# Key blocks of 128 within one batch, one PSUM bank per batch for the value products, maxima taken off by small products

## The chip, the cores and the metric

The kernel runs on one core of one Trainium2 chip. The time is the device time of one execution of the whole program, in microseconds; a kernel is given as the median of several runs. The engines are PE (TensorE, matrix products into PSUM), DVE (VectorE), ACT (ScalarE), POOL (GpSimd) and SP, which here only issues DMAs. PSUM is the accumulator memory in front of PE: eight banks, each of 512 fp32 values per partition, 128 partitions.

## The reference

q, k and v are float32 arrays of 8 batches x 12 heads x 448 rows x 64. The result of the attention is the input of a soft mixture of experts.

```python
scores = scale * np.matmul(q, k.transpose(0, 1, 3, 2))
m = np.max(scores, axis=-1, keepdims=True)
e = np.exp(scores - m)
attn = e / (np.sum(e, axis=-1, keepdims=True) + np.exp(-m) + 1e-09)
x = np.matmul(attn, v)          # then heads side by side: 3584 rows of 768
logits = x @ phi                # 32 slots, 4 for each of 8 experts
d = exp(logits - logits.max(0)); d /= d.sum(0) + 1e-09
slot_input = d.T @ x            # each expert: relu(slot_input @ w1) @ w2
c = exp(logits - logits.max(1)); c /= c.sum(1) + 1e-09
out = c @ slot_out
```

## The kernel before

The attention is cut into 24 units of two batches and two heads (the heads lie on the two partition halves of the transposed q and k). A row of 448 is seven blocks of 64 (TB = 7), or three of 128 and one of 64 (C3 = 3). One loop runs over steps; seven steps belong to a unit, and several units are in flight. Each step issues one score tile for the maxima of unit u (`stage_S`, L208) and, LAG = 11 steps later, one tile of transposed scores of the same unit (`stage_ST`, L242). Everything else hangs in a plan: `at(n, place, f)` puts a stage at a step, and within a step the order is "small", S, "mid", "value", ST, "end", "load" (L571 to 580). Every engine and each DMA queue works off its instructions in that written order.

The stages of a unit, with n its first step:

- `load_qk`, `load_v` (L114, L120): q and k come through POOL's queue, cast to bf16; v comes as float32 through SP's queue, two DMAs. `load_w` brings a piece of the expert weights through POOL's queue.
- `stage_T` (L194): 28 transposes of q and k of the next unit into a PSUM tile of two banks; DVE copies q (L204), then ACT copies k (L205).
- `stage_S`: four products of 64 stationary columns (two heads x two halves of 64 rows) over 448 keys; DVE reduces the two banks to row maxima (L219), which go to a tile M.
- `stage_MT` (L221, step n + 7): M is transposed by PE, copied by ACT (`mt`), exponentiated for the denominator (`em`), and POOL multiplies `mt` with a mask to `md` (L231, L237): for each batch and head a matrix of 64 x 448 whose column sum is minus the maximum of each row.
- `stage_ST`: for 64 keys of both batches, four products of a column of ones with `md` (L247) and four products of k and q (L252) add up to scores minus maxima; ACT takes the exponential (L256) into one of four buffers `et`.
- `stage_V` (L259, step n + 10): POOL casts v to bf16 beside a column of ones.
- `stage_AV` (L266): `et` times v, 64 keys of each batch at a time: 16 products of 65 columns per t, batch 0 on the upper and batch 1 on the lower row half, summed over t in a PSUM tile of two banks. AV0 gives the step of each t after n.
- `stage_AVout`, `stage_shift`, `stage_N` (L289 to L322): ACT copies the sums to the single buffer `xu` (L293, L296), POOL moves the half blocks (L304) and adds up the denominator, DVE takes reciprocals, POOL multiplies (L319).
- `stage_X` (L327, step n + 27): seven transposes, copied by DVE (L332), for the mixture's logits.

After each six units `mixture` works on the 768 features of a batch pair, in steps of its own, from 28 steps after the last of these units began. PSUM is given out by `slot` (L94): four slots of two banks, r0 to r3, each request taking the slot that is due first; the value products hold theirs from the first t to the copy. After the loop come the experts and the output (from L583).

## Time and profile before

| | |
|---|---|
| median of 3 runs | 354.83 us (351.5, 354.83, 356.85) |
| span of the profiled execution | 351.5 us |
| time of the profiled execution | equal to the lowest run, 351.5 us |
| busy: PE, DVE, POOL, ACT | 279.6, 245.8, 230.8, 223.1 us |
| one undisturbed unit (from 147.51 us on) | 9.86 us |
| main loop, last score tile | 268.75 us |
| mixture's last logits | 290.46 us |
| first output rows | 321 us |

Busy time is the union of an engine's instructions. PE's matrix products are pipelined: one row shows a product from its start to the modelled end, so the lengths of neighbours overlap, and what a group costs PE is the distance to the next start. A releaser in brackets is what ended the idle time before an instruction.

### The profile page before, as it was taken

How to read it: one execution, taken by the hardware profiler on the slowest of the kernel's cores; microseconds unless marked ns; L12 is line 12 of the kernel's file. 1: busy time of each engine (PE TensorE's matmuls, PEld its weight loads, DVE VectorE, ACT ScalarE, POOL GpSimd, SP SyncE). 2: the span in 40 equal slices, each digit the busy share in tenths (PEclk: the TensorE clock that was granted, in tenths of full speed). 3: DMA queues.
4: the chain of work that ended last, by engine and by line, in shares of the span. 5: the costliest groups of instructions: out<-in, count | busy, mean ns of one | idle time of the engine just before them, and what ended most of it. 6: DMA issues, size and time to landing. Idle time of an engine off the chain costs nothing.

```text
span 351.5 us, 14003 instructions
## 1 busy us (share of the span) xinstructions
PE 279.6 (80%) x6152; PEld 159.8 (45%) x6152; DVE 245.8 (70%) x321; ACT 223.1 (63%) x353; POOL 230.8 (66%) x413
## 2 busy tenths in 40 slices
PE   2679898998989789999968987899689745877760
PEld 1334554564555455556545544555455423342110
DVE  1886887988787978889888876878987015207440
ACT  1236887787778488888777776877588832015340
POOL 8335688899886878999876878698757573210000
PEclk9999999999999999999999999999999975596555
DMA  7455379789988898899997799869956599963997
GB/s 92 80 96 100 54 146 202 115 162 185 186 168 167 139 209 158 140 170 174 169 178 146 109 222 205 163 96 183 176 121 113 125 168 205 216 133 149 395 399 313
DMA packets 30061, 59.14 MB, mean 168 GB/s; under 512 B 4049, under 2 KB 22225, under 8 KB 30001
## 3 DMA queue, kind: packets, MB, share of 16 engines
q0 software_dynamic: 19344, 36.69, 61.7%
q1 hardware_dynamic: 10656, 21.57, 18.7%
q8 instruction: 48, 0.79, 0.9%
q14 instruction: 13, 0.10, 0.1%
HBM read 83.46 MB, written 11.01 MB: 269 GB/s over the span
## 4 chain that ended last, share of the span: by engine, by line
PE 31%; ACT 13%; DMA 12%; DVE 12%; issue 8%; POOL 6%; SPq 3%; ACTq 0%; POOLq 0%; DVEq 0%
PE ps L282 12%; ACT block L256 9%; PE ps L216 7%; DVE m L219 6%; PE ps L247 6%; DMA block<-in_moe_w_dram 5%; PE ps L252 4%; SPq L635 3%; DMA block<-in_v_dram 3%; DMA block<-in_k_dram 2%; DVE block L204 2%; DMA out_dram<-wres 2%; DVE sm L431 2%; ACT block L205 1%; POOL block L319 1%
## 5 line engine op out<-in xcount | busy, mean ns | idle before, releaser
L219 DVE TENSOR_REDUCE m<-ps 128x2 bf16<-128x896 f32 x168 | 179.5, 1090 | 41.4 <-PE ps L216 33.5
L256 ACT ACTIVATE block<-ps 128x896 bf16<-128x896 f32 x168 | 154.3, 922 | 49.9 <-PE ps L252 47.2
L216 PE MATMUL ps<-block 64*64 64x448 bf16 x672 | 66.6, 382 | 21.5 <-ACT block L205 12.0
L282 PE MATMUL ps<-block 64*128 64x65 bf16 (+1 forms) x2688 | 73.1, 196 | 4.2 <-issue 2.0
L282 PEld LDWEIGHTS <-block 64*128 64x128 bf16 (+1 forms) x2688 | 53.0, 97 | 42.6 <-issue 29.5
L247 PE MATMUL ps<-block,ones 64*64 64x448 bf16 x672 | 64.5, 364 | 5.4 <-ACT cT L445 2.4
L252 PE MATMUL ps<-block 64*64 64x448 bf16 x672 | 63.4, 356 | 0.0
L216 PEld LDWEIGHTS <-block 64*64 64x64 bf16 x672 | 32.3, 108 | 53.5 <-issue 37.4
L319 POOL TENSOR_TENSOR block<-block,rec 128x896 bf16<-128x896 f32 (+1 forms) x24 | 40.1, 1672 | 4.5 <-DVE rec L313 4.5
L304 POOL COPY block<-block 64x65 f32<-64x65 f32 x96 | 22.6, 236 | 26.5 <-ACT block L296 23.5
L231 POOL TENSOR_TENSOR block<-mt,nmask 128x768 bf16<-128x768 bf16 x24 | 36.0, 1502 | 3.9 <-ACT mt L225 2.7
L110 POOL DMA_DIRECT2D block<-in_q_dram x46 | 29.4, 640 | 14.0 <-PE ps L203 10.5
L205 ACT COPY block<-ps 128x896 bf16<-128x896 bf16 x24 | 21.8, 907 | 23.8 <-DVE block L204 23.8
L110 POOL DMA_DIRECT2D block<-in_k_dram x46 | 27.8, 618 | 2.0 <-issue 2.0
L247 PEld LDWEIGHTS <-ones 64*64 64x64 bf16 x672 | 23.5, 107 | 12.1 <-issue 7.4
L261 POOL CAST block<-block 128x896 bf16<-128x896 f32 x24 | 22.6, 941 | 5.8 <-DMA block<-in_v_dram 5.8
L203 PE MATMUL ps<-ident,block 128*64 128x128 bf16 x644 | 24.1, 228 | 2.0 <-DMA block<-in_q_dram 1.0
L203 PEld LDWEIGHTS <-block 128*64 128x64 bf16 x644 | 20.8, 115 | 8.2 <-issue 6.0
L252 PEld LDWEIGHTS <-block 64*64 64x64 bf16 x672 | 21.3, 109 | 0.9
L332 DVE COPY block<-ps 128x896 bf16<-128x896 bf16 x24 | 14.8, 616 | 9.7 <-PE ps L330 9.7
L293 ACT COPY block<-ps 128x780 f32<-128x780 f32 x24 | 19.5, 813 | 3.1 <-PE ps L282 2.0
L630 PE MATMUL ps<-wres,cT 32*128 32x384 bf16 x56 | 17.6, 493 | 4.5 <-DVE wres L633 2.5
(105 smaller groups left out, 254.4 us busy)
## 6 DMA issues: line engine op xcount, KB each, us to landing
wres<-in_moe_w_dram POOLq DMA_DIRECT2D x23, 768.0 KB, 7.7
out_dram<-wres SPq DMA_DIRECT2D x28, 384.0 KB, 4.2
block<-in_v_dram SPq DMA_DIRECT2D x46, 224.0 KB, 7.2
block<-in_moe_w_dram POOLq DMA_DIRECT2D x9, 768.0 KB, 12.8
block<-in_q_dram POOLq DMA_DIRECT2D x46, 112.0 KB, 4.8
block<-in_k_dram POOLq DMA_DIRECT2D x46, 112.0 KB, 4.5
block<-in_v_dram POOLq DMA_DIRECT2D x2, 224.0 KB, 4.2
wres<-in_q_dram POOLq DMA_DIRECT2D x2, 112.0 KB, 3.1
```

The lines of the kernel that those rows point to most:

```text
L110: eng.dma_start(out=t_[ds(b * P, P), :, :], in_=src[bp * 2 + b, ds(hp * 2, 2)].rearrange("h (p t) d -> p h (t d)", t=TB))
L203: nc.tensor.transpose(o[i][ds(h * D, D), :, ts(t, P)], r[:, h, ts(t, D)], ident)
L205: nc.scalar.copy(t_[:, 1], o[1])
L216: nc.tensor.matmul(ps[ds(r * P, P), h, ds(0, S)], QT[u][hs, b, ds(o, P)], KT[u][hs, b, :], start=True, stop=True)
L219: nc.vector.tensor_reduce(m[:, :, s], ps[:, :, ds(0, S)], axis=AX.X, op=ALU.max)
L231: nc.gpsimd.tensor_tensor(md[:, :, ds(0, C3 * 128)].rearrange("p b (c n) -> p b c n", c=C3), mt.unsqueeze(1).unsqueeze(1).broadcast_to([12 ...
L247: nc.tensor.matmul(ps[ds(b * P, P), h, ds(0, S)], ones[hs, :], MD[u][hs, b, :], start=True, stop=False)
L252: nc.tensor.matmul(ps[ds(b * P, P), h, ds(0, S)], KT[u][hs, b, ds(t * P, P)], QT[u][hs, b, :], start=False, stop=True)
L256: nc.scalar.activation(et, ps[:, :, ds(0, S)], AF.Exp, scale=scale)
L261: nc.gpsimd.tensor_copy(t_[:, :, :, ds(0, D)], RAW.pop((u, "vr")).rearrange("p h (t d) -> p h t d", t=TB))
L282: nc.tensor.matmul(o, et[bs, h, ds(c * 128, w)], V65[u][bs, h, t, ds(0, 65)], start=(t == 0 and h == 0 and c == 0), stop=(t == TB - 1), sk ...
L319: eng.tensor_tensor(xo[:, hs], xv[:, hs, :, ds(0, D)], rec[:, hs].unsqueeze(3).broadcast_to([128, nh, TB, D]), op=ALU.mult)
```

## The change

Keys are taken in blocks of 128 of one batch: t = 0 to 2 are batch 0, t = 4 to 6 batch 1, and t = 3 is the half block of 64 keys of both. So that the halves lie together, k is transposed into another column order (KPOS) and v is loaded by four DMAs instead of two. The scores for the maxima take 128 stationary columns, two products instead of four. In `stage_ST` the maxima are taken off by products of a column of the mask (broadcast to 128 columns) with `mt` itself, 128 or 64 columns each: eight per tile, sixteen for t = 3. POOL's two products with the mask and the tiles `md` go. The value products have 128 keys and are half as many for t other than 3; each batch has one PSUM bank, copied out on its own at steps n + 16 and n + 19. PSUM becomes three slots of two banks (r0 to r2) and two of one bank (a0, a1), the latter for value sums and, where free, other small tiles. The column of ones beside v is set once. The denominator takes two additions instead of one, the normalization three products instead of one. LAG is 9, the value products stand at n + 13, n + 15 and n + 18, `stage_X` at n + 25 and the mixture starts two steps sooner; the late weight loads move by one or two steps.

```diff
-LAG = 11
-AV0 = (15, 16, 16, 17, 18, 19, 19)
+LAG = 9
+AV0 = (13, 13, 15, 15, 18, 18, 18)
+AVO = (16, 19)
...
-                          ("vr", 2 * N2, 1), ("md0", N2, 1), ("v65", 2 * TB * 66, 1),
-                          ("qk2", 2 * N2, 1), ("md1", N2, 1), ("v66", 2 * TB * 66, 1),
-                          ("et", N2, 4), ("xu", 4 * TB * 65, 1), ("xq", 4 * 65, 1),
+                          ("vr", 2 * N2, 1), ("v65", 2 * TB * 66, 1),
+                          ("qk2", 2 * N2, 1), ("v66", 2 * TB * 66, 1),
+                          ("et", N2, 6), ("xu", 4 * TB * 65, 1), ("xq", 2 * 65, 1),
...
-    LAGS = {"S": 3, "ST": 3.5, "T": 3, "X": 2.5, "M": 3, "held": 3.5}
-    due, made, where = [0.0] * 4, [0], {}
+    LAGS = {"S": 3, "ST": 3.5, "T": 3, "X": 2.5, "M": 3}
+    due = {f"r{i}": 0.0 for i in range(3)} | {f"a{i}": 0.0 for i in range(2)}
+    made, held = [0], []
...
-        i = min(range(4), key=lambda j: (due[j], j))
-        due[i] = made[0] + LAGS.get(kind, 2) if kind != "hold" else float("inf")
-        where[kind] = i
-        return psum.tile(shape, dtype, tag=f"r{i}", name="ps")
+        one = mybir.dt.size(dtype) * shape[1] * (shape[2] if len(shape) > 2 else 1) <= 2048
+        small_ = [i for i in ("a0", "a1") if one and (kind == "AV" or due[i] <= made[0] + 1)]
+        i = min(small_ or ("r0", "r1", "r2"), key=lambda j: (due[j], j))
+        if kind == "AV":
+            assert due[i] < float("inf")
+            held.append(i)
+            due[i] = float("inf")
+        else:
+            due[i] = made[0] + LAGS.get(kind, 2)
+        return psum.tile(shape, dtype, tag=i, name="ps")
...
-        due[where["hold"]] = made[0] + LAGS["held"]
+        due[held.pop(0)] = made[0] + 3
...
-        RAW[u, "vr"] = load(u, t_, v, nc.sync if u else nc.gpsimd)
+        bp, hp = divmod(u, HP)
+        for b in range(2):
+            src = v[bp * 2 + b, ds(hp * 2, 2)].rearrange("h (p t) d -> p h (t d)", t=TB)
+            for r, t0, t1, at_ in ((0, 0, C3 + 1 - b, b * (C3 + 1)), (1, C3 + 1 - b, TB, b * C3)):
+                (nc.sync if u else nc.gpsimd).dma_start(
+                    out=t_[ds(r * P, P), :, ds(at_ * D, (t1 - t0) * D)],
+                    in_=src[:, :, ds(t0 * D, (t1 - t0) * D)])
+        RAW[u, "vr"] = t_
...
+    for i in range(2):
+        nc.vector.memset(buf(f"v6{5 + i}", 0).rearrange("p (n e) -> p n e", e=66)[:, :, ds(D, 1)], 1.0)
...
-    QT, KT, MD, ET, EM, AV, XU, X, DEN = {}, {}, {}, {}, {}, {}, {}, {}, {}
+    KPOS = (0, 2, 4, 6, 1, 3, 5)
+    QT, KT, NM, ET, EM, AV, XU, X, DEN = {}, {}, {}, {}, {}, {}, {}, {}, {}
...
-                    nc.tensor.transpose(o[i][ds(h * D, D), :, ts(t, P)], r[:, h, ts(t, D)], ident)
+                    nc.tensor.transpose(o[i][ds(h * D, D), :, ts(KPOS[t] if i else t, P)],
+                                        r[:, h, ts(t, D)], ident)
...
         ps = slot([128, 2, 512], kind="S")
         for h in range(2):
             hs = ds(h * D, D)
-            for r in range(2):
-
-                b, o = divmod(s, C3) if s < 2 * C3 else (r, C3)
-                o = o * 128 + (r * P if s < 2 * C3 else 0)
-                nc.tensor.matmul(ps[ds(r * P, P), h, ds(0, S)], QT[u][hs, b, ds(o, P)],
+            if s < 2 * C3:
+                b, c = divmod(s, C3)
+                nc.tensor.matmul(ps[:, h, ds(0, S)], QT[u][hs, b, ts(c, 128)],
+                                 KT[u][hs, b, :], start=True, stop=True)
+                continue
+            for b in range(2):
+                nc.tensor.matmul(ps[ds(b * P, P), h, ds(0, S)], QT[u][hs, b, ds(C3 * 128, P)],
                                  KT[u][hs, b, :], start=True, stop=True)
         m = M[u % 2].rearrange("p (h r) -> p h r", h=2)
         nc.vector.tensor_reduce(m[:, :, s], ps[:, :, ds(0, S)], axis=AX.X, op=ALU.max)
...
     def stage_MT(u):
         ps = slot([128, 128], BF16, "M")
         nc.tensor.transpose(ps, M[u % 2], ident)
-        mt = small.tile([128, 128], BF16, tag="mt", name="mt", bufs=1)
+        mt = small.tile([128, 128], BF16, tag="mt", name="mt")
         nc.scalar.copy(mt, ps)
-        em = small.tile([128, 2, TB], F32, tag="em", name="em")
+        em = small.tile([128, 2, TB], F32, tag="em", name="em", bufs=3)
         nc.scalar.activation(em, M[u % 2].rearrange("p (h r) -> p h r", h=2)[:, :, ds(0, TB)],
                              AF.Exp, scale=-scale)
         EM[u] = em
-        md = buf(f"md{u % 2}", 0).rearrange("p (b n) -> p b n", b=2)
-        nc.gpsimd.tensor_tensor(
-            md[:, :, ds(0, C3 * 128)].rearrange("p b (c n) -> p b c n", c=C3),
-            mt.unsqueeze(1).unsqueeze(1).broadcast_to([128, 2, C3, 128]),
-            nmask[:, ds(0, 2 * C3)].rearrange("p (b c) -> p b c", b=2).unsqueeze(3)
-                 .broadcast_to([128, 2, C3, 128]),
-            op=ALU.mult)
-        nc.gpsimd.tensor_tensor(
-            md[:, :, ds(C3 * 128, P)], mt.rearrange("p (b n) -> p b n", b=2),
-            nmask[:, ds(2 * C3, 1)].unsqueeze(2).broadcast_to([128, 2, P]), op=ALU.mult)
-        MD[u] = md
+        NM[u] = mt
     def stage_ST(u, t):
         ps = slot([128, 2, 512], kind="ST")
-        for b in range(2):
+        b, c = divmod(t, C3 + 1)
+        blocks = [(b, slice(0, 128), ts(c, 128))] if t != C3 else [
+            (b, ds(b * P, P), ds(C3 * 128, P)) for b in range(2)]
+        for q in range(C3 + 1):
+            for b, rows, ks in blocks:
+                for h in range(2):
+                    hs = ds(h * D, D)
+                    i, cs = (b * C3 + q, ds(0, 128)) if q < C3 else (2 * C3, ds(b * P, P))
+                    m = NM[u][hs, cs]
+                    nc.tensor.matmul(ps[rows, h, ds(q * 128, m.shape[1])],
+                                     nmask[hs, ds(i, 1)].broadcast_to([D, P * 2 // len(blocks)]), m,
+                                     start=(q == 0), stop=False, skip_group_check=True)
+        for b, rows, ks in blocks:
             for h in range(2):
                 hs = ds(h * D, D)
-                nc.tensor.matmul(ps[ds(b * P, P), h, ds(0, S)], ones[hs, :], MD[u][hs, b, :],
-                                 start=True, stop=False)
-        for b in range(2):
-            for h in range(2):
-                hs = ds(h * D, D)
-                nc.tensor.matmul(ps[ds(b * P, P), h, ds(0, S)],
-                                 KT[u][hs, b, ds(t * P, P)], QT[u][hs, b, :],
-                                 start=False, stop=True)
+                nc.tensor.matmul(ps[rows, h, ds(0, S)], KT[u][hs, b, ks], QT[u][hs, b, :],
+                                 start=False, stop=True, skip_group_check=True)
         et = buf("et", u * TB + t).rearrange("p (h n) -> p h n", h=2)
         nc.scalar.activation(et, ps[:, :, ds(0, S)], AF.Exp, scale=scale)
         ET[u, t] = et
...
         t_ = buf(f"v6{5 + u % 2}", 0).rearrange("p (h t e) -> p h t e", h=2, e=66)
         nc.gpsimd.tensor_copy(t_[:, :, :, ds(0, D)],
                               RAW.pop((u, "vr")).rearrange("p h (t d) -> p h t d", t=TB))
-        nc.gpsimd.memset(t_[:, :, :, ds(D, 1)], 1.0)
         V65[u] = t_
     def stage_AV(u, ts_, part):
-
-
-
         for t in ts_:
-            if t == 0 and part == 0:
-                AV[u] = slot([128, 2, 512], kind="hold")
-            av, et = AV[u], ET[u, t]
+            et = ET[u, t]
+            bs = (0, 1) if t == C3 else (t // (C3 + 1),)
+            if part == 0 and t in (0, C3):
+                AV[u, bs[-1]] = slot([128, 512], kind="AV")
             for h in range(2):
                 for c in (range(C3) if part == 0 else (C3,)):
-                    for b in range(2):
-                        bs = ds(b * P, P)
+                    for b in bs:
+                        av = AV[u, b]
+                        ks = ds(b * P, P) if t == C3 else slice(0, 128)
                         if c < C3:
-                            o, w = av[:, b, ds((h * C3 + c) * 65, 65)], 128
+                            o, w = av[:, ds((h * C3 + c) * 65, 65)], 128
                         else:
-                            o, w = av[ds(h * P, P), b, ds(2 * C3 * 65, 65)], P
-                        nc.tensor.matmul(o, et[bs, h, ds(c * 128, w)],
-                                         V65[u][bs, h, t, ds(0, 65)],
-                                         start=(t == 0 and h == 0 and c == 0),
-                                         stop=(t == TB - 1), skip_group_check=True)
+                            o, w = av[ds(h * P, P), ds(2 * C3 * 65, 65)], P
+                        nc.tensor.matmul(o, et[ks, h, ds(c * 128, w)],
+                                         V65[u][ks, h, t, ds(0, 65)],
+                                         start=(t == (C3 if b else 0) and h == 0 and c == 0),
+                                         stop=(t == (TB - 1 if b else C3)), skip_group_check=True)
             if part == 1:
                 ET.pop((u, t))
-    def stage_AVout(u):
-        av = AV.pop(u)
-        xu = buf("xu", 0).bitcast(F32).rearrange("p (h s e) -> p h s e", h=2, e=65)
-        xq = buf("xq", 0).bitcast(F32).rearrange("p (b e) -> p b e", b=2)
-        nc.scalar.copy(
-            xu[:, :, ds(0, 2 * C3), :].rearrange("p h (b c) e -> p b h (c e)", b=2),
-            av[:, :, ds(0, 2 * C3 * 65)].rearrange("p b (h e) -> p b h e", h=2))
-        nc.scalar.copy(xq, av[:, :, ds(2 * C3 * 65, 65)])
-        XU[u] = xu, xq
+    def stage_AVout(u, b):
+        xu = buf("xu", 0).bitcast(F32).rearrange("p (b n) -> p b n", b=2)
+        nc.scalar.copy(xu[:, b], AV.pop((u, b))[:, ds(0, TB * 65)])
+        XU[u] = xu.rearrange("p b (s e) -> p b s e", e=65)
         release()
     def stage_shift(u):
-        xu, xq = XU[u]
-        for h in range(2):
-            for b in range(2):
-                nc.gpsimd.tensor_copy(xu[ds(b * P, P), h, TB - 1, :], xq[ds(h * P, P), b, :])
+        xu = XU[u]
+        xq = buf("xq", 0).bitcast(F32)
+        R = 2 * C3
+        nc.gpsimd.tensor_copy(xq[ds(0, P)], xu[ds(P, P), 0, R])
+        nc.gpsimd.tensor_copy(xu[ds(P, P), 0, R], xu[ds(0, P), 1, R])
+        nc.gpsimd.tensor_copy(xu[ds(0, P), 1, R], xq[ds(0, P)])
         den = small.tile([128, 2, TB], F32, tag="den", name="den")
-        nc.gpsimd.tensor_tensor(den, xu[:, :, :, D], EM.pop(u), op=ALU.add)
+        em = EM.pop(u)
+        nc.gpsimd.tensor_tensor(
+            den[:, :, ds(0, R)].rearrange("p b (h c) -> p b h c", h=2),
+            xu[:, :, ds(0, R), D].rearrange("p b (h c) -> p b h c", h=2),
+            em[:, :, ds(0, R)].rearrange("p h (b c) -> p b h c", b=2), op=ALU.add)
+        nc.gpsimd.tensor_tensor(den[:, :, R], xu[:, :, R, D], em[:, :, R], op=ALU.add)
         nc.gpsimd.tensor_scalar(den, den, 1e-9, None, op0=ALU.add)
         DEN[u] = den
     def stage_N(u):
-        xv = XU.pop(u)[0]
+        xv = XU.pop(u)
+        R = 2 * C3
         rec = small.tile([128, 2, TB], F32, tag="rec", name="rec", bufs=1)
         nc.vector.reciprocal(rec, DEN.pop(u))
         x = buf("x", u + 4).rearrange("p (s n) -> p s n", s=TB)
-        xo = x.rearrange("p s (h d) -> p h s d", h=2)
-        for h0, nh, eng in (((0, 2, nc.gpsimd),) if u < U - 1 else
-                            ((0, 1, nc.gpsimd), (1, 1, nc.vector))):
-            hs = ds(h0, nh)
+        for b in range(2):
+            eng = nc.vector if b and u == U - 1 else nc.gpsimd
             eng.tensor_tensor(
-                xo[:, hs], xv[:, hs, :, ds(0, D)],
-                rec[:, hs].unsqueeze(3).broadcast_to([128, nh, TB, D]), op=ALU.mult)
+                x[:, ts(b, C3)].rearrange("p c (h d) -> p h c d", h=2),
+                xv[:, b, ds(0, R), ds(0, D)].rearrange("p (h c) d -> p h c d", h=2),
+                rec[:, b, ds(0, R)].rearrange("p (h c) -> p h c", h=2).unsqueeze(3)
+                   .broadcast_to([128, 2, C3, D]), op=ALU.mult)
+        nc.gpsimd.tensor_tensor(
+            x[:, R].rearrange("p (h d) -> p h d", h=2), xv[:, :, R, ds(0, D)],
+            rec[:, :, R].unsqueeze(2).broadcast_to([128, 2, D]), op=ALU.mult)
         X[u] = x
...
-        at(n + 19, "value", lambda u=u: stage_AVout(u))
-        at(n + 19, "end", lambda u=u: stage_shift(u))
-
-        at(n + (22 if u % HP == 1 else 21), "end" if u % HP == 1 else "mid",
+        for b in range(2):
+            at(n + AVO[b], "value", lambda u=u, b=b: stage_AVout(u, b))
+        at(n + AVO[1], "end", lambda u=u: stage_shift(u))
+        at(n + AVO[1] + (3 if u % HP == 1 else 2), "end" if u % HP == 1 else "mid",
...
-        at(n + 27, "value", lambda u=u: stage_X(u))
+        at(n + 25, "value", lambda u=u: stage_X(u))
...
-        mixture(bp, (bp * HP + HP - 1) * TB + 28, at)
+        mixture(bp, (bp * HP + HP - 1) * TB + 26, at)
...
-    for n, i in ((end - 4, 0), (end + 3, 1), (end + 10, 2), (end + 12, 3), (end + 12, 4),
-                 (end + 15, 5), (end + 21, 6), (end + 28, 7), (end + 28, 8)):
+    for n, i in ((end - 5, 0), (end + 3, 1), (end + 9, 2), (end + 11, 3), (end + 11, 4),
+                 (end + 15, 5), (end + 19, 6), (end + 26, 7), (end + 26, 8)):
```

More of the change, by code (lines that the diff above doesn't have):

```diff
@@ L152 @@
     load_qk(1)
-    ones = const.tile([128, P], BF16, name="ones")
-    nc.vector.memset(ones, 1.0)
     nmask = const.tile([128, TB], BF16, name="nmask")
```

## The prediction

> **What bounds it now.** I read the page's busy shares first, because they leave the question open:
>
> ```profile
> PE 279.6 (80%) x6152; PEld 159.8 (45%) x6152; DVE 245.8 (70%) x321; ACT 223.1 (63%) x353; POOL 230.8 (66%) x413
> ```
>
> No engine is full, so I laid the timelines of one undisturbed unit side by side. On PE (columns: start us, length, what; in brackets the idle time before it and its releaser):
>
> ```profile
> 147.51 0.38 PE L216 MATMUL ps<-block 64*64 64x448 bf16 x4 [0.54 <-ACT block L205]
> 148.33 0.38 PE L216 MATMUL ps<-block 64*64 64x448 bf16 x4
> 148.65 0.51 PE L282 MATMUL ps<-block 64*128 64x65 bf16 x16
> 149.16 0.38 PE L247 MATMUL ps<-block,ones 64*64 64x448 bf16 x4
> 149.54 0.39 PE L216 MATMUL ps<-block 64*64 64x448 bf16 x4
> 149.86 0.72 PE L282 MATMUL ps<-block 64*128 64x65 bf16 x32
> 150.41 0.36 PE L247 MATMUL ps<-block,ones 64*64 64x448 bf16 x4
> 150.81 0.38 PE L216 MATMUL ps<-block 64*64 64x448 bf16 x4
> ...
> 154.35 0.36 PE L216 MATMUL ps<-block 64*64 64x448 bf16 x4
> 154.68 0.97 PE L203 MATMUL ps<-ident,block 128*64 128x128 bf16 x28
> 155.58 0.56 PE L330 MATMUL ps<-ident,block 128*128 128x128 bf16 x7
> 156.09 0.38 PE L247 MATMUL ps<-block,ones 64*64 64x448 bf16 x4
> ...
> 157.37 0.38 PE L216 MATMUL ps<-block 64*64 64x448 bf16 x4 [0.54 <-ACT block L205]
> ```
>
> See that a unit lasts 157.37 - 147.51 = 9.86 us. Call its score matmuls S0 to S6 (L216); they start 0.82, 1.21, 1.27, 1.23, 1.06 and 1.25 us apart, then 3.02 to the next S0. Lengths overlap, so costs are differences of starts: S holds PE 0.19, a whole ST (L247 and L252) 0.39, 16 value products with their surroundings 0.33, 32 of them 0.55: 0.22 per 16, 13.75 ns each. S to value products takes 0.32 where S to ST takes 0.19, so **a change of tile shape costs 0.13**. DVE and ACT in the same unit:
>
> ```profile
> 148.01 1.10 DVE L219 TENSOR_REDUCE m<-ps 128x2 bf16<-128x896 f32 x1 [0.96 <-PE ps L216]
> 149.17 6.69 DVE L219 TENSOR_REDUCE m<-ps 128x2 bf16<-128x896 f32 x6
> 155.76 0.61 DVE L204 COPY block<-ps 128x896 bf16<-128x896 bf16 x1
> 156.30 0.61 DVE L332 COPY block<-ps 128x896 bf16<-128x896 bf16 x1
> ```
>
> ```profile
> 149.84 0.92 ACT L256 ACTIVATE block<-ps 128x896 bf16<-128x896 f32 x1 [0.48 <-PE ps L252]
> 156.41 0.91 ACT L205 COPY block<-ps 128x896 bf16<-128x896 bf16 x1 [0.37 <-DVE block L204]
> ```
>
> Three links follow. An exponential starts 0.68 after its ST and lets an S into its slot 0.97 after that (149.84 to 150.81), so S(s+2) cannot start before ST(s) + 1.63. A reduction lets the next ST in 1.15 after it starts (148.01 to 149.16). And T, Q copy, K copy, S0 is a chain in which the X copy fills a hole of DVE. The value products of five steps fit because each adds 0.46 or 0.68 to a step that the first link holds near 1.2 anyway. **PE's order and these slots set the end**, not one engine's sum. POOL is near full too:
>
> ```profile
> 149.80 1.51 POOL L231 TENSOR_TENSOR block<-mt,nmask 128x768 bf16<-128x768 bf16 x1
> 151.23 0.43 POOL L237 TENSOR_TENSOR block<-mt,nmask 128x128 bf16<-128x128 bf16 x1
> 155.28 1.06 POOL L304 COPY block<-block 64x65 f32<-64x65 f32 x4 [0.28 <-ACT block L296]
> ```
>
> but it still waits for ACT there, and PE waits for POOL 1.8 us in the whole run.
>
> **Part by part.** *POOL.* The two products go (1.94 us a unit), with a memset (0.16) and one shift copy (0.24); the split N and denominators add 0.6. POOL falls from 9.4 to about 7.7 us. Nothing on PE waited for these, so by itself this is worth nothing in a regular unit; it moves the V cast and the SP loads behind it about 1.5 us earlier, while the value products use V two steps sooner (0.82 to 1.25 each).
>
> *Streams.* S as two products of 128 columns instead of four of 64 runs the same 448 columns on both halves: 0.19. Value products with 128 keys: columns on X's row take 56 ns per 128 (7 in 0.39), so 65 take 28 ns; six such and two half-wide ones are 0.20 per step where 16 took 0.22. Halving the count buys 0.14 a unit, since two row halves already ran at once. The bound above is X's 56 ns if the load of weights does not hide: +1.3 a unit. I take 28, as the value row's 13.75 on half the rows is the nearest.
>
> *Small products.* Six of 128 and two of 64 columns, on two row halves, replace four of 448 on four quarters: the same 448 columns per half, 0.19. The trace has no such product on a broadcast weight column. Below, 0.17 (columns alone); above, 56 ns each as X's, one at a time: 0.39, 0.20 more per ST. I take 0.19, by the value row, whose pairs of load and product cost 13.75 ns. The Trainium skill ("TensorE: Matmul & The Clock Gate", Back-to-back issue gap) gives 81 ns as the sustained spacing of a load and product of 128 columns; by it, as an estimate, the eight would take 0.57 us and the unit some 2 us more. X's 56 and the transposes' 27 ns here speak against it.
>
> *Changes of shape.* Before: two for each of five value steps, five around T, X and M: 15. After, five in the step of t = 2, 3 (the middle block is split), four with t = 4 to 6 and X, three with t = 0, 1 and T, two for M, one for block 3: 15 again. Changes of rows only are not in the trace: 0 to 0.13; I take 0.13, the row of S to value products.
>
> *Slots.* Following the rule of `slot` through the plan, S, ST and T go round r0 to r2: as before, ST(s) takes the slot of S(s-1) and S(s+1) that of ST(s-1). The links stay. What moves is the work between them: value products of five steps now sit in three, X leaves T's step for that of t = 4 to 6, and t = 0, 1 sits ahead of T.
>
> *The unit again, S to S:*
> S0-S1 0.82 as now (exponential behind the K copy).
> S1-S2: 0.19, products 0.42, five changes 0.65, ST 0.39 = 1.65 (now 1.21).
> S2-S3: 1.63 - 0.39 = 1.24 (1.27).
> S3-S4: the exponential before, 0.81, the first bank's copy (455 columns by the 780 and 130 rows: 0.54, 0.44 behind another), then 0.97: 1.25 (1.23). That copy also overwrites what N of the unit before reads. N starts after the reciprocal, 1.7 after S0, and takes 2.1 in three pieces (rows of 896 and 448 elements); ACT is ready for the copy at 3.5 and waits 0.3, with the exponential and S4 behind it: 1.55.
> S4-S5: 0.19, value 0.59, X 0.39, four changes 0.52, ST 0.39 = 2.08 (1.06).
> S5-S6: 1.24 (1.25); the second copy fits.
> S6-S0: value 0.39 and three terms 0.19 + 0.26 bring T to 0.84 instead of 0.33; Q copy 1.03 after T, at 1.87 instead of 1.41; from it 1.61 as now = 3.48 (3.02).
> Sum 12.06 against 9.86: **+2.2 a unit**. DVE loses too: the X copy (0.53) no longer fills the hole, but it is then not last.
>
> *The run.* 14 regular units: +31. Their present excess over 9.86 (some 6 us, code and transfers) half hides: -3. The six units with a mixture lie 16.6 above 9.86 in all; their logits and slot products now fall into steps 5 and 6, where PE waits: 6 x 2.2 - 8 = +5. The unit that waits for q and k (12.2) changes by nothing. The end has two ST steps less (0.82 each) and no product on POOL: -4. Together +29 on the profiled execution's span of 351.5, which is also the lowest of the three runs, so nothing lies around it: 380.5. The median shown is 3.3 higher; I add that: **384**.
>
> *Transfers.* v goes from two to four issues a unit on SP (two took 1.25, so 1.25 more) with runs half as long. Last landing plus cast, 1.9 + 7.2 + 0.95, is 10.1, over 9.86 but under 12.06: hidden by the longer unit; without it, 0.2 a unit. The cast ends near 5.5 after S0 and t = 0 is multiplied near 9, so V is in time. The late weight loads move with their steps and keep their order on POOL's queue: nothing. K's new column order and the third `em` buffer add no instruction.
>
> **Rivals.** *Small products one at a time* (bound above): 0.2 in five steps, 1.0 a unit, 404. For: nothing like them is traced. Against: the value row.
> *POOL set the pace.* POOL works 9.4 of 9.86, and DMA stalls near 204 and 268 hang on its late issues. Then PE's sum without waits (9.86 - 0.54 - 0.28 = 9.04) is next: -0.8 in 21 units and -4 at the end: 334, faster. It decides if S4-S5 stays under 1.3, that is if the clusters fill PE's idle time. Against: S waits in the trace name ACT and DVE.
> *Clusters partly absorbed.* Row changes free (0.13 twice in S1-S2, twice in S4-S5, 0.52 a unit), the wait for N absent (0.3), and the mixtures giving back all 16.6: +1.4 in 14 units, -8 in the six, -3 and -4 as above: 359.
> *v late.* With two weight loads together v landed in 10.5; if halved runs make that usual, 0.95 + 1.9 + 10.5 = 13.3 a unit: 412.
>
> **Numbers.** Forecast 0.52 (own range 370 to 396), small products 0.11, POOL 0.18, absorbed 0.14, v late 0.05. 2% (348 to 362) is about what these runs, 1.5% apart, can tell. Faster 0.18; same 0.10 (two thirds of absorbed); slower 0.72, the rest. The range leaves out most of the POOL case and v late: 346 to 404.
>
> **What would show it.** Right: PE gaps near 2.1 and 1.65 where t = 4 to 6 and t = 2, 3 lie, S0 to S0 near 12, DVE's hole at the unit's end 1.5 instead of 0.96, ACT's first copy waiting for N, POOL below 60%. Wrong: S4-S5 under 1.5, or shape changes well under 0.13 would break the sum; ST above 0.5 is the first rival; a V cast waiting for its load in most units the last.

## The result, and the profile after

The changed kernel takes 396.87 us (median of 4 runs, 395.25 to 398.36), the kernel before on the same chip 354.60 us (351.5 to 356.85): a ratio of 1.1225 with an interval of 1.1158 to 1.1291. The forecast was 384, with a range of 346 to 404 and 370 to 396 for its main case. The profiled execution, the longest of the four, took 398.36 us; its span is 396.6 us (before 351.5). Some executions of a program are slower by up to a few per cent whatever the kernel; they stand in no ratio below, but the profiles of two kernels (v in four DMAs, transposes earlier) show such an execution. The engines' shares, on the page of the changed kernel:

```profile
PE 293.2 (74%) x5288; PEld 178.0 (45%) x5288; DVE 245.8 (62%) x322; ACT 219.6 (55%) x353; POOL 189.8 (48%) x390
```

POOL lost 41 us of work, PE gained 14, DVE has the same 245.8 and ACT 3.5 less; all four now stand idle for more of the time. One undisturbed unit on PE, from the timeline of the changed kernel (start us, length, what, and in brackets the idle time and its releaser):

```profile
166.54 0.36 PE L231 MATMUL ps<-block 64*128 64x448 bf16 x2 [1.00 <-ACT block L222]
...
167.36 0.37 PE L231 MATMUL ps<-block 64*128 64x448 bf16 x2
167.66 0.95 PE L295 MATMUL ps<-block 128*128 128x65 bf16 x24
168.54 0.37 PE L262 MATMUL ps<-mt,nmask 64*128 64x128 bf16 x8
168.75 0.35 PE L268 MATMUL ps<-block 64*128 64x448 bf16 x2
168.94 0.35 PE L231 MATMUL ps<-block 64*128 64x448 bf16 x2
...
170.17 0.36 PE L231 MATMUL ps<-block 64*128 64x448 bf16 x2 [0.35 <-ACT block L271]
...
171.75 0.36 PE L231 MATMUL ps<-block 64*128 64x448 bf16 x2 [0.70 <-ACT block L271]
172.05 0.93 PE L295 MATMUL ps<-block 128*128 128x65 bf16 x24
172.91 0.56 PE L349 MATMUL ps<-ident,block 128*128 128x128 bf16 x7
...
173.81 0.35 PE L231 MATMUL ps<-block 64*128 64x448 bf16 x2
...
175.04 0.38 PE L235 MATMUL ps<-block 64*64 64x448 bf16 x4 [0.37 <-ACT block L271]
175.36 0.72 PE L295 MATMUL ps<-block 128*128 128x65 bf16 x16
175.91 0.95 PE L219 MATMUL ps<-ident,block 128*64 128x128 bf16 x28
```

The next unit's S0 starts at 178.52, so a unit is 11.98 us; before it was 9.86. See the two long steps: from 167.36 to 168.94 there are 24 value products between two scores, from 171.75 to 173.81 there are 24 value products and X. And see the long way from 175.04 to 178.52. On DVE and ACT the same unit shows:

```profile
167.01 1.10 DVE L238 TENSOR_REDUCE m<-ps 128x2 bf16<-128x896 f32 x1 [1.46 <-PE ps L231]
```

```profile
165.58 0.91 ACT L222 COPY block<-ps 128x896 bf16<-128x896 bf16 x1 [1.32 <-DVE block L221]
170.34 0.54 ACT L304 COPY block<-ps 128x455 f32<-128x455 f32 x1 [0.22 <-POOL block L338]
```

DVE's hole at the unit's start has grown from 0.96 to 1.46, and ACT's copy of the first batch's sums (L304) waits 0.22 for the last piece of N of the unit before (L338). ACT's copy of k waits for DVE's copy of q, as before; that line comes back below.

Not all units are like this one. Irregular units are measured here and below from one M (PE's transpose of a unit's maxima) to the next. From the M at 228.86 to that at 246.31 it takes 17.45 us, and there the chain of work that ended last (start us, length, what) says why:

```profile
224.60 9.80 DMA block<-in_v_dram
234.40 0.02 issue
234.42 7.41 DMA block<-in_v_dram
...
242.00 0.92 POOL block L276
...
242.96 1.07 PE ps L295 x14
```

Two landings of v, one after the other (the second pair of DMAs is issued 0.02 us after the first has landed), then the cast, then the value products. The waits in SP's DMA queue (total us, times, longest), first of the kernel before and then of the changed one:

```profile
SPq L110 <- DMA block<-in_v_dram: 123.7, 23, 10.7
```

```profile
SPq L134 <- DMA block<-in_v_dram: 158.9, 50, 13.1
```

One wait for a landing per unit has become two.

### The profile page after: what moved, and what is told of

It is laid out like the page before. It is cut to its first block, busy times and chain, and to the rows that moved or that the text cites. A ratio compares the mean times of both kernels' runs of the same rounds, so it can differ in the third digit from the quotient of the medians.

```text
span 396.6 us, 12319 instructions
## 1 busy us (share of the span) xinstructions
PE 293.2 (74%) x5288; PEld 178.0 (45%) x5288; DVE 245.8 (62%) x322; ACT 219.6 (55%) x353; POOL 189.8 (48%) x390
## 4 chain that ended last, share of the span: by engine, by line
PE 30%; DMA 17%; POOL 16%; ACT 14%; issue 13%; DVE 8%; SPq 0%; POOLq 0%; ACTq 0%; DVEq 0%
PE ps L295 10%; ACT block L271 9%; DMA block<-in_v_dram 8%; POOL block L333 5%; DMA block<-in_moe_w_dram 4%; PE ps L231 4%; DMA out_dram<-wres 4%; PE ps L219 4%; POOL block L118 4%; PE ps L262 3%; DVE m L238 3%; ACT block L222 3%; PE ps L349 3%; DVE block L221 2%; PE ps L268 2%
## 5 line engine op out<-in xcount | busy, mean ns | idle before, releaser
L231 PE MATMUL ps<-block 64*128 64x448 bf16 x288 | 55.5, 381 | 52.4 <-ACT block L271 27.6
L295 PE MATMUL ps<-block 128*128 128x65 bf16 (+3 forms) x1536 | 67.3, 203 | 9.6 <-POOL block L276 9.0
L295 PEld LDWEIGHTS <-block 128*128 128x128 bf16 (+3 forms) x1536 | 52.3, 103 | 34.0 <-issue 21.7
L262 PE MATMUL ps<-mt,nmask 64*128 64x128 bf16 (+3 forms) x1536 | 66.3, 221 | 1.1 <-DVE m L238 1.0
L268 PE MATMUL ps<-block 64*128 64x448 bf16 (+1 forms) x384 | 64.4, 374 | 0.0
L262 PEld LDWEIGHTS <-nmask 64*128 64x128 bf16 (+1 forms) x1536 | 48.0, 102 | 31.2 <-issue 20.5
L231 PEld LDWEIGHTS <-block 64*128 64x128 bf16 x288 | 22.2, 97 | 74.3 <-issue 67.8
L333 POOL TENSOR_TENSOR block<-block,rec 128x384 bf16<-128x384 f32 x47 | 38.0, 828 | 22.3 <-DVE rec L329 20.1
L313 POOL COPY block<-block 64x65 f32<-64x65 f32 x24 | 5.6, 234 | 65.0 <-ACT block L304 64.8
L276 POOL CAST block<-block 128x896 bf16<-128x896 f32 x24 | 22.5, 936 | 24.1 <-DMA block<-in_v_dram 21.4
L304 ACT COPY block<-ps 128x455 f32<-128x455 f32 x48 | 25.7, 536 | 9.6 <-POOL block L338 9.3
L652 DVE COPY wres<-ps 128x768 f32<-128x768 f32 x14 | 13.3, 957 | 10.3 <-DMA out_dram<-wres 8.9
```

The source lines that it names most:

```text
L231: nc.tensor.matmul(ps[:, h, ds(0, S)], QT[u][hs, b, ts(c, 128)], KT[u][hs, b, :], start=True, stop=True)
L262: nc.tensor.matmul(ps[rows, h, ds(q * 128, m.shape[1])], nmask[hs, ds(i, 1)].broadcast_to([D, P * 2 // len(blocks)]), m, start=(q == 0), s ...
L268: nc.tensor.matmul(ps[rows, h, ds(0, S)], KT[u][hs, b, ks], QT[u][hs, b, :], start=False, stop=True, skip_group_check=True)
L295: nc.tensor.matmul(o, et[ks, h, ds(c * 128, w)], V65[u][ks, h, t, ds(0, 65)], start=(t == (C3 if b else 0) and h == 0 and c == 0), stop=(t ...
L304: nc.scalar.copy(xu[:, b], AV.pop((u, b))[:, ds(0, TB * 65)])
L333: eng.tensor_tensor(x[:, ts(b, C3)].rearrange("p c (h d) -> p h c d", h=2), xv[:, b, ds(0, R), ds(0, D)].rearrange("p (h c) d -> p h c d", ...
```

## The experiments

Two theories stood at the start. The forecast's own: the order of the work on PE makes the units longer, that is value products in clusters (those of two or three key tiles in one step), the first copy of sums in a bad place and T behind value products. The second is for the 16 us by which the span of 396.6 lies above the 380.5 of the forecast: v is loaded in two rounds. The POOL rival and that of dear small products were tested beside them. Each median is to be read beside that of the kernel before on the same chip (355.1, 355.5, 355.0 and 355.5 us). The score starts S0 to S6 of one undisturbed unit, worked out from the PE timelines:

| kernel | S0-S1 | S1-S2 | S2-S3 | S3-S4 | S4-S5 | S5-S6 | S6-S0 | unit |
|---|---|---|---|---|---|---|---|---|
| before | 0.82 | 1.21 | 1.27 | 1.23 | 1.06 | 1.25 | 3.02 | 9.86 |
| after, forecast | 0.82 | 1.65 | 1.24 | 1.55 | 2.08 | 1.24 | 3.48 | 12.06 |
| after, measured | 0.82 | 1.58 | 1.23 | 1.58 | 2.06 | 1.23 | 3.48 | 11.98 |
| later copy | 0.82 | 1.58 | 1.24 | 0.80 | 2.06 | 1.24 | 3.47 | 11.21 |
| spread | 1.13 | 1.24 | 1.12 | 1.72 | 1.63 | 1.24 | 3.26 | 11.34 |
| before, clusters | 0.82 | 1.25 | 1.25 | 1.25 | 1.25 | 1.46 | 3.02 | 10.30 |
| all taken back | 1.13 | 1.23 | 1.12 | 1.15 | 1.84 | 1.24 | 3.05 | 10.76 |
| keys apart as well | 1.13 | 1.23 | 1.12 | 1.15 | 1.84 | 1.24 | 2.43 | 10.14 |

### Value products spread, in the changed kernel

```diff
-AV0 = (13, 13, 15, 15, 18, 18, 18)
+AV0 = (13, 14, 15, 16, 17, 18, 19)
```

> The changed kernel with AV0 = (13, 14, 15, 16, 17, 18, 19), one value product step per step, nothing else. Theory of the clusters: S1-S2 falls from 1.57 to 1.24, S4-S5 from 2.05 to 1.69 (X is still there), S6-S0 from 3.47 to 3.29, S0-S1 rises from 0.82 to 1.17, S3-S4 to 1.7; the unit goes from 11.98 to about 11.5 us and the run to about 386. Rival, the value products' place does not matter and v's loads or POOL set the unit: 11.98 again, 394 to 399. If shape changes cost more than the 0.13 that the trace shows, it gets slower: five more of them a unit, over 400.

Measured: 398.68 us, ratio 1.1226 (1.1125 to 1.1328). The unit fell by 0.64 to 11.34, as the clusters' cost says, and the span from the first M to the last from 297.1 to 286.7. The time didn't move, because of one wait in the end:

```profile
334.12 0.68 PE L295 MATMUL ps<-block 128*128 128x65 bf16 x8 [14.83 <-DMA block<-in_moe_w_dram]
```

With the last t one step later, its products of the last unit stand behind a weight load that takes over their operands' place. They wait 14.83 us for it and then multiply weights instead of exponentials, so this kernel's last unit is computed wrongly and only its times are of use. Without that wait it would be some 384 us by the wait alone, or 388 with the changed kernel's end (81.7 us from the last M, here 92.8); both are estimates, 386 was expected. So spreading is worth about 0.6 us per unit.

### The first copy one step later

```diff
-AVO = (16, 19)
+AVO = (17, 19)
```

> The changed kernel with AVO = (17, 19): the first bank is copied one step later, when the normalization of the unit before has read the buffer. Theory of the new wait: S3-S4 falls from 1.58 to about 1.25, the unit from 11.98 to 11.7, and the units in which POOL is late lose their longer stall as well: 386 to 390. Rival, the wait is covered by something that is as late: no change, 395 to 398.

Measured: 376.74 us, ratio 1.0594 (1.0523 to 1.0665). S3 and S4 of an undisturbed unit:

```profile
163.88 0.37 PE L231 MATMUL ps<-block 64*128 64x448 bf16 x2 [0.36 <-ACT block L271]
164.68 0.37 PE L231 MATMUL ps<-block 64*128 64x448 bf16 x2
```

They are 0.80 apart where they were 1.58, and S4 waits for nothing. The wait for N (0.22) is the smaller part: the copy itself (0.54) had stood in the chain from ST(2) to S4, and one step later it fits behind an exponential that nobody waits for. Wait and copy, 0.22 and 0.54, are the 0.77 of the unit. The gain of 20 us is more than 0.77 in each of 23 units gives (18). The second unit after each mixture's start gained 3 to 4 us (10.44, 10.62 and 10.62 for 14.50, 13.57 and 13.85), while another lost 3.4 to a late v (16.33 for 12.96). The expectation had only counted the wait.

### The kernel before with v in four DMAs

```diff
-        RAW[u, "vr"] = load(u, t_, v, nc.sync if u else nc.gpsimd)
...
+        for b in range(2):
...
+            for t0, t1 in ((0, 4), (4, TB)):
+                (nc.sync if u else nc.gpsimd).dma_start(
+                    out=t_[ds(b * P, P), :, ds(t0 * D, (t1 - t0) * D)],
+                    in_=src[:, :, ds(t0 * D, (t1 - t0) * D)])
...
```

> The kernel before with v loaded by four DMAs of half the row length instead of two, nothing else. Theory of two rounds (SP issues the second pair only when the first has landed): from one cast to the next it takes two landings of about 5 us and the cast of 0.95, some 11.5 us against a unit of 9.86, so the casts wait and the unit rises by 0.8 to 1.6: 370 to 390. Rival, short rows alone cost: one landing of 7.3 plus 1.25 of issue, hidden in 9.86 but for 0.2 a unit: 354 to 360.

Measured: 440.9 us (one run). Far past both expectations. SP waits 47 times for a landing, 166.1 us in all, POOL's cast 131.4 us in 22 units, and most units are 15 to 19 us. Shorter rows alone don't explain this: in one unit SP issues the four DMAs at 165.91, 168.50, 169.14 and 174.22. Each batch's second DMA, which goes to the same rows of the tile as its first, is issued when the first has landed, so a unit's v takes three landings in a row here and not two. What makes one DMA wait for another was the next thing to find.

### The second pair on POOL's queue, in the changed kernel

```diff
-                (nc.sync if u else nc.gpsimd).dma_start(
+                (nc.gpsimd if b or not u else nc.sync).dma_start(
```

> The changed kernel with the second pair of its four value loads on GpSimd's queue, so that the four are under way together. If the second round of loads makes the sixteen microseconds that the forecast missed, the waits of the value cast (21.4 us in ten) mostly go, no unit of 16 to 17 us is left, and the time falls from 397 to 382 to 388 us. If the transfers are late because the weight loads share the DMA engines, 394 to 400 us; if the two DMAs hold GpSimd's queue back, above 400 us.

Measured: 466.39 us, ratio 1.31 (1.3003 to 1.3197), in the last of the expected ranges. That one queue lets only two DMAs through at a time, another possible cause, falls too. On POOL's timeline:

```profile
165.41 1.30 POOL L134 DMA_DIRECT2D block<-in_v_dram  x2 [9.04 <-DMA block<-in_v_dram]
```

The pair on another queue waits for the first pair all the same, and now POOL waits with it: 156.9 us in 24 units, with the shifts, the denominators and N behind it. The Trainium skill ("DMA: Bandwidth & Descriptors", "Anatomy of one DMA — SWDGE (gpsimd) path") states that a DMA's semaphore wait happens on the issuing sequencer, not in the DMA engines; the trace agrees, with those 9.04 us of POOL. So the wait seems to belong to the data, which the next kernel tests. Both pairs write the same rows of one tile, and by head their strips interleave: t 0 to 3 of head 0, t 4 to 6 of head 0, t 0 to 3 of head 1, and so on. No value is written twice, but the program orders the pairs as if it were.

### Strips that don't interleave

```diff
-                    out=t_[ds(r * P, P), :, ds(at_ * D, (t1 - t0) * D)],
+                    out=t_[ds(r * P, P), ds(2 * at_ * D, 2 * (t1 - t0) * D)]
+                        .rearrange("p (h n) -> p h n", h=2),
```

with the cast of V in four pieces, one by strip (2.43 us of POOL for 0.92).

> The changed kernel with its value loads still on SP's queue, but the strips of the raw values laid out so that the two batches' strips of the same rows are two separate stretches of columns, and not interleaved by head; the cast becomes four casts by strip. Theory: the second pair waits for the first because the strips interleave, whatever the queue. Then the waits of SP on landings fall from 50 to about 25, the value cast waits little, no unit is 16 to 17 us, and the time is 382 to 388 us. Rival: the waits come from how many loads are under way at once; then 50 waits stay, with 394 to 402 us. If the four casts (some 2.0 us for 0.95) hold GpSimd, above 400 us.

Measured: 386.9 us, ratio 1.0915 (1.085 to 1.098), as expected. In SP's queue:

```profile
SPq L134 <- POOL block L280: 183.6, 63, 11.1
SPq L134 <- DMA block<-in_v_dram: 84.3, 22, 10.5
```

SP's four issues of one unit, in the changed kernel and then with separate strips:

```profile
160.73 5.94 SPq L134 DMA_DIRECT2D block<-in_v_dram  x4
```

```profile
159.61 2.66 SPq L134 DMA_DIRECT2D block<-in_v_dram  x4
```

The waits for a landing are back at one a unit, SP waits for POOL's casts instead, and one cast alone waits for v (2.9 us): the unit of 17.45 us is 11.97, that of 16.37 is 13.72. All four DMAs are issued within 2.66 us, before any has landed, so it is not only that four casts free the strips earlier. Regular units stay at 11.98. So the two rounds cost 11.5 us of span (396.6 to 385.1; 10.0 between the medians), most of it in these two units, and the interleaving was their cause.

### The small products

First in the kernel before, with POOL's two products gone and sixteen small products per ST:

```diff
-        md = buf(f"md{u % 2}", 0).rearrange("p (b n) -> p b n", b=2)
-        nc.gpsimd.tensor_tensor(
...
-        MD[u] = md
+        MD[u] = mt
...
-                nc.tensor.matmul(ps[ds(b * P, P), h, ds(0, S)], ones[hs, :], MD[u][hs, b, :],
-                                 start=True, stop=False)
+        for g in range(C3 + 1):
...
+                    nc.tensor.matmul(ps[ds(b * P, P), h, ds(g * 128, m.shape[1])],
+                                     nmask[hs, ds(i, 1)].broadcast_to([D, P]), m,
+                                     start=(g == 0), stop=False, skip_group_check=True)
```

> The kernel before with the maxima taken off by sixteen small products of the mask column and mt (64 stationary columns each) in every transposed score tile, and without POOL's two products; the rest as before. My theory: the small products cost PE 0.02 to 0.04 a tile (0.22 for sixteen in the changed kernel's trace against 0.19) and POOL's 1.94 us a unit were not what the unit waited for: 350 to 358, no change. Rival, POOL set the pace: 0.8 less a unit, 330 to 340. Rival, small products run one at a time: 0.2 more in five steps of a unit, over 370.

Measured: 401.83 us, ratio 1.1282 (1.1175 to 1.1389), 46 us off and over 370, but not for the reason that was expected there. The small products did not take longer (0.20 from their first to the next product). But PE now stops ahead of products with no releaser in the profile:

```profile
170.36 0.36 PE L240 MATMUL ps<-block,nmask 64*64 64x128 bf16 x13 [0.66 <-issue]
174.63 0.37 PE L276 MATMUL ps<-block 64*128 64x65 bf16 x7 [0.75 <-issue]
```

23.5 us of such waits stand before small products and 16.4 before value products. This kernel has 17,984 instructions where the one before has 14,003 and the changed one 12,319, and its instruction queue moved 1.05 MB (0.79 and 0.67). That PE ran out of instructions is a reading that fits; no run tests it apart. One unit, from the S0 at 28.43 on, has no such wait, and its steps are those of an undisturbed unit of the kernel before: 9.88 us for 9.86. So there the small products cost nothing, and POOL's lighter load (47% of the span) gained nothing. A second test takes the small products out of the changed kernel (L256 to L264, and the sum starts at L268), so that the maxima are not taken off:

> The changed kernel without its small products: the maxima are not taken off, so the exponentials are those of the bare scores. 0.19 us of TensorE goes from each of 168 score steps, 1.3 us per unit. If TensorE's order is the bound all through the unit, all of it comes back: 397 - 30 = 367 us. If only the three steps with clusters and the end of the unit are TensorE's, about half: 380 to 390 us. If the second round of value loads sets the pace beside them, 392 us or more.

Measured: 405.75 us, ratio 1.1425 (1.1366 to 1.1483): slower with 1536 products less, and slower than the changed kernel, for which no expectation had a cause. Units at full clock are 11.78, that is 0.20 shorter of the 1.33 us that the products take on PE; in the steps that wait for ACT they cost nothing. That the run is longer all the same goes with a lower granted clock. The windows table (window, length, then busy us and instructions of PE, PEld, DVE, ACT, POOL, the granted clock, DMA share, GB/s), without small products and then the changed kernel:

```profile
17.00:115.00 98.00, 73.38 (x937) 40.06 (x933) 67.12 (x74) 59.02 (x88) 50.26 (x101) 0.82 0.66 116
```

```profile
17.00:115.00 98.00, 76.43 (x1532) 48.07 (x1527) 71.23 (x79) 63.03 (x95) 53.71 (x110) 1.00 0.70 125
```

### Clusters alone, in the kernel before

```diff
-AV0 = (15, 16, 16, 17, 18, 19, 19)
+AV0 = (15, 15, 17, 17, 19, 19, 19)
```

> The kernel before with its value products gathered in two, two and three key tiles (steps 15, 17 and 19) in place of one, two, one, one, two. If a cluster between two score products costs by itself, as the forecast has it (a unit's steps with three tiles near 2.1 us, those without near 0.8), the unit is about 0.46 us longer: 355 + 0.46 x 23 = 365 us (361 to 370). If TensorE has room for it and ScalarE and VectorE set the pace, 352 to 358 us.

Measured: 361.38 us, ratio 1.0165 (1.0101 to 1.0229). The unit is 10.30, 0.44 longer, where 0.46 was expected; the run lost 6 us and not 10. The steps are not as expected (2.1 with three tiles, 0.8 with none): those with two tiles and those with none are 1.25 alike, the step with three is 1.46. A step cleared of products doesn't get shorter, as ACT's exponential holds its score. That is how a cluster costs although PE does the same work.

### Transposes earlier, in the kernel before

```diff
-            at(n + 6, "mid", lambda u=u: stage_T(u + 1))
+            at(n + 6, "small", lambda u=u: stage_T(u + 1))
```

> The kernel before with the next unit's transposes ahead of the last score product of a unit, and not behind it. The first scores of a unit wait 0.5 us for ScalarE's copy of the keys, and VectorE idles 0.96 us there; with the copies a step earlier 0.3 to 0.5 us of each of 23 units go: 343 to 349 us. If the last reduction of the unit, then later by the transposes, takes the place of the copies, 352 to 358 us; if the transposes hold the PSUM that the last scores need, 360 us or more.

Measured: 356.55 us, ratio 1.0002 (0.995 to 1.0054): nothing, the second of the expectations. The copies come earlier, and the last reduction, behind DVE's copy of q, is what M waits for instead (0.41 us).

### All of it taken back

A first kernel had the spread products, the later copy, the transposes ahead of the first value products, and the pair on POOL's queue:

> The changed kernel with four of its costs taken back at once: value products spread over six steps, the first copy of sums one step later, the transposes of the next unit ahead of the first value products, the second pair of value loads on GpSimd's queue; both the product shapes and the small products stay. If the order of the work and the loads make the loss, the regular unit is 10.2 to 10.6 us (11.98 in the changed kernel, 9.86 before) and the time 356 to 367 us. If the gains overlap with what the later copy gained alone (377), 368 to 376 us. If the small products and shapes themselves cost, it can't come below 375 us.

Measured: 457.58 us, ratio 1.2897 (1.2791 to 1.3003); the pair on POOL's queue undid the rest, as above. With separate strips in its place:

```diff
-AV0 = (13, 13, 15, 15, 18, 18, 18)
-AVO = (16, 19)
+AV0 = (13, 14, 15, 16, 17, 18, 18)
+AVO = (17, 19)
...
-            at(n + m, "mid", lambda u=u, m=m: [
+            at(n + m, "value" if m == AV0[0] else "mid", lambda u=u, m=m: [
```

> The changed kernel with those separate strips, value products spread over six steps, the first copy of sums one step later, and the transposes of the next unit ahead of the first value products. If order and loads make the loss, the regular unit is about 10.1 to 10.3 us and the time 352 to 362 us, beside 355 of the kernel before. If the loads' two rounds stay, 368 us or more.

Measured: 353.64 us against 354.98, ratio 0.9967 (0.9934 to 1.0). So nearly all of the 42 us came from the order and the loads; the new shapes and the small products are still in this kernel. The regular unit is 10.76, above the expected 10.1 to 10.3 and 0.9 above the old one, but its mixture units are shorter in sum (12.95 and 10.64 from M to M, where the kernel before has 12.61 and 13.63). What holds its S0 is a wait that all these kernels share:

```profile
147.64 0.61 DVE L222 COPY block<-ps 128x896 bf16<-128x896 bf16 x1
148.29 0.91 ACT L223 COPY block<-ps 128x896 bf16<-128x896 bf16 x1 [0.89 <-DVE block L222]
...
149.25 0.36 PE L232 MATMUL ps<-block 64*128 64x448 bf16 x2 [0.67 <-ACT block L223]
```

ACT's copy of k waits for DVE's copy of q, which it doesn't need. Both read one PSUM tile. With a tile of its own for k:

```diff
         ps = slot([128, 2, 1024], BF16, "T")
+        ps2 = slot([128, 1024], BF16, "T")
...
-        o = [ps[:, i, ds(0, N2)].rearrange("p (b n) -> p b n", b=2) for i in range(2)]
+        o = [x.rearrange("p (b n) -> p b n", b=2) for x in (ps[:, 0, ds(0, N2)], ps2[:, ds(0, N2)])]
```

> The changed kernel with all its costs taken back as above, and the transposes of the keys in a PSUM tile of their own, so that ScalarE's copy of the keys need not wait for VectorE's copy of the queries. In that kernel's unit of 10.75 us the copy waited 0.89 us for the queries' copy, and the first scores 0.67 us for the copy; with both copies beside each other the first scores come 0.5 to 0.65 us earlier in some 20 units: 341 to 346 us, 3% under the kernel before. If ScalarE's or VectorE's order takes the gain, 350 to 356 us; if the keys' tile collides with the value products' PSUM, above 358 us.

Measured: 342.87 us against 355.52, ratio 0.9652 (0.9623 to 0.9681), as expected: faster than both kernels.

```profile
150.79 0.91 ACT L224 COPY block<-ps 128x896 bf16<-128x896 bf16 x1
150.90 0.62 DVE L223 COPY block<-ps 128x896 bf16<-128x896 bf16 x1
...
151.90 0.36 PE L233 MATMUL ps<-block 64*128 64x448 bf16 x2
```

The copies run side by side, S6 to S0 takes 2.43 where it took 3.05, and S0 waits for nothing.

## Why the prediction was right, and where it was not

**The unit: right, step by step.** All seven distances came within 0.07 of the forecast, the sum 11.98 for 12.06. The trace bears out the small products (0.19 to 0.21 from their first to the next product, 0.19 forecast), the value products (24 in 0.88 with the change of shape, from 167.66 to 168.54), and DVE's hole (1.46 for 1.5). The 81 ns of the Trainium skill ("TensorE: Matmul & The Clock Gate", "Back-to-back issue gap"), which the forecast weighed, would by the forecast's estimate have made the eight small products 0.57; the trace does not agree, with 0.19 to 0.21. The change of shape by rows only, put at 0.13, is 0.11: S to value products takes 0.30 where S to ST takes 0.19.

**The wait of the copy: right place, part of its price.** Forecast 0.3, measured 0.22. The copy itself is in the forecast's sum for S3-S4 (0.44 behind an exponential), but that sum without the wait, 1.25, is near the old 1.23, and so the place of the copy looked harmless. The later copy shows 0.80, and 1.25 less 0.44 is 0.81: the copy was the larger part of what its place cost.

**The run: right without v.** Leave v out by the kernel with separate strips: from the first M to the last it takes 287.4 us, before 253.2, so +34.2 where the forecast had 31 - 3 + 5 = +33. The six mixture units alone are +5.1 (82.8 for 77.7; forecast +5).

**The end: -4 came as -1.** From the last M to the end of the span it is 81.0 before and 80.0 with separate strips. Up to the last of the logits' products it is 20.1 us for 21.5, and the weight load that the end then waits for took 18.55 for 17.82. Why the first is shorter by 1.3 and not by 4 stays open.

**v: the step that failed.** The forecast had "last landing plus cast, 1.9 + 7.2 + 0.95, is 10.1 ... hidden by the longer unit", with 1.25 added for two more issues. It took the four DMAs as under way together. They went in two rounds: in the unit from 228.86 the chain has 9.80, 7.41 and 0.92, which no unit of 12 hides. This is 11.5 us, and with the end (2.9), the stream (1.2) and the start (0.5) it makes up the 16.1 by which the span of 396.6 lies above the forecast's 380.5. The forecast's step from the span to the time was off too: it let nothing lie between the two, as in the one run of 351.5, where most other runs show some 2 us (398.36 for 396.6). The 396.87 lies just outside the main case's 370 to 396 and inside the whole range. In all, 10 of the 24 casts waited for a landing (21.4 us), so the sign that the forecast had named for it, a cast that waits in most units, did not come. The rival "v late" had the place and not the mechanism: it made v a cost of every unit, 412 us, for loads made slow by shorter runs.

**The other rivals.** "Small products one at a time" falls by the row above. "POOL set the pace" falls: POOL is at 48% and the unit is longer, and the kernel of 342.87 us runs with POOL at 65%. (The forecast's own reading, that PE waits 1.8 us for POOL in the whole run before, holds for the value products only; X waits another 4.8 us for N, 4.5 of it once.) "Clusters partly absorbed" falls for the regular unit (10.30 in the kernel before with clusters alone) and holds in part for the run (6 us lost where 0.44 in each of 23 units would be 10).

## What to carry to other kernels

Read the cost of a rearranged order from the distances between the starts on the engine that sets the pace, one step at a time: steps that something else holds near a fixed length give nothing back when they are cleared, while a crowded step pays in full. When one load is cut into several, look at whether the pieces' strips interleave in their tile before you add up issue times; each pair that the program must keep in order costs a whole landing. And look for waits between readers of one tile: a copy that waits for another copy of the same tile is a dependency of the layout, not of the data.

## What the hardware showed that was not expected

**A lower clock for less work.** Without its small products PE's granted clock was 0.82, 0.81 and 0.80 in three windows of the loop (1.00, 0.96 and 0.88 in like windows of the changed kernel). This is a mean: in units of 13.07 us the step with 24 value products and X took 3.11 us, in those of 11.78 it took 1.86, and in a few units 28 transposes took some 1.7 us, in most 0.95. Between 17 and 115 us no wait of PE on another engine was longer than 1.5 us. The Trainium skill ("TensorE: Matmul & The Clock Gate", "A second HAM failure mode: psum-queue depth-cycling") states that frequent short idle times between groups of products let the clock swing between half and full rate; the trace agrees with that in direction. That those gaps are the cause was not tested apart: the exponentials there are of other values, too. The kernel of 342.87 us kept 1.00 all through the loop, with PE busy 94% of it.

**The same after a long wait.** In the changed kernel PE stood 3.98 us for v, and the transposes right behind took 1.69 us instead of 0.95; from 246 to 275 us the clock was 0.77. A late load can be paid twice.

```profile
242.96 1.07 PE L295 MATMUL ps<-block 128*128 128x65 bf16 x16 [3.98 <-POOL block L276]
...
243.83 1.69 PE L219 MATMUL ps<-ident,block 128*64 128x128 bf16 x28
```
